# A hand-made order for the head of a linear-attention and SwiGLU kernel, with six zero matmuls fewer

## The chip, the cores and the metric

The kernel runs on one core of one Trainium2 chip. The metric is the device time of one execution in microseconds (us). The times before are 200.81, 200.97 and 201.14, median 200.97.

A core has five engines, each with its own queue that it works through in order: TensorE (PE, matrix products into PSUM), VectorE (DVE), ScalarE (ACT), GpSimd (POOL) and SyncE (SP, which here only issues transfers). [...]

## The reference

A recurrence with a decaying state per head (B = 4 batches, H = 8 heads, S = 768 steps, D = 48), then an RMS norm and a gated feed-forward layer (384 to 1536 to 384).

```python
for t in range(S):
    cur = np.einsum('bhd,bhe->bhde', u[None] * kt, vt)
    y[:, :, t] = np.einsum('bhd,bhde->bhe', rt, state + cur)
    state = wt[:, :, :, None] * state + np.einsum('bhd,bhe->bhde', kt, vt)
...
xn = x / rms * rms_g
g = xn @ w_gate
silu = g * (1.0 / (1.0 + np.exp(-g)))
val = xn @ w_val
return (silu * val @ w_out).astype(np.float32)
```

## The kernel before

The 768 steps are cut into six superblocks of 128 steps. A superblock n has four batches j, and its recurrence is computed as masked matrix products. The feed-forward part works on a whole superblock, 4 x 128 = 512 rows at a time, in twelve chunks f of 128 hidden units.

Every step is a small function `fn(n, j)`, and the text constant `ORDER` names all 1086 of them as `fn.n.j`. At its end the kernel runs through that list and calls them, so that this one list sets the order on every engine:

```python
    for step in ORDER.split():
        fn, n, j = step.split(".")
        fns[fn](int(n), int(j))
```

The same list decides the PSUM banks. Three rings, `a` and `b` of two banks and `q` of four, are handed out by `psum`, which takes the bank whose last use lies furthest back in `ORDER`.

The steps for one batch of a superblock, with the engine and the line that the profile shows:

- `load_r`, `load_k`, `load_v` (L248) and `load_w` (L261): transfers, issued on SP.
- `ln` (ACT), `cs_mm` (PE, L402 to L409), `exp_r` and `exp_k` (ACT): the cumulated decay. In superblock 0 the exponentials stay in PSUM; in superblock 1 they are written to SBUF as `er` and `ek`.
- `r_mul` (L455) and `k_mul` (L461), DVE: r and k times the decay, into `rk`. `w_tot` (L446), DVE.
- `rk_pe` (PE, L484) and `rk_tr` (ACT, L493): the transpose of `rk`, and its copy into `rkT`.
- `q_mm` (PE, L502 and L504): the score products; `q_mask_e` (L509) and `q_mask_o` (L517), DVE: their masks, into `qts`.
- `bonus_mul` (POOL, L467 and L468, two products of about 1.0 us), `bonus_sum` (DVE, L472), `bonus_v` (POOL, L477): the u term, into `ydiag`.
- `x_pe` (PE, L557) puts `ydiag` into the output bank; `y_mm` (PE, L552) adds the score products.
- `x_sq` (L570), `x_rstd`, `xn_mul` (L585), ACT: the norm. `xn_pe` (PE, L596) and `xn_out` (DVE, L607): the transpose of the normed rows into `xnt`.
- `cast_v` (ACT, L379), `st_mm` (PE, L530), `st_new` (DVE, L537): the state for the next superblock.

When `xn_out` of all four batches is done, the feed-forward part can start: `gate_mm` and `val_mm` (PE, L626, three matmuls each), `silu` (ACT), `h_mul` (DVE, L658), and later `o_mm` (PE, L672). `load_gv.g.h` (L351) and `load_wo` (L357) bring the weights in; they are issued on POOL, whose queue they share with the products above. `gate_mm.0.0` needs `load_gv.0.0`; chunks 4 to 11 need `load_gv.1.0` and `load_gv.1.1`.

`warm` (L374) is a matmul of zeros whose result nobody reads. There are 13 at the start (L285), outside the list, and 36 in the list, all in superblock 0's part. The step's first number counts them and has no other meaning.

The head, in this text, is the stretch up to the first `gate_mm` and `val_mm` of superblock 0, about the first 36 us. In it the list mixes steps of superblock 0 with the first ones of superblock 1.

Of the kernel before, what the change touches and what calls it, by code (L numbers as in the profile page):

```python
# [25 lines left out]
load_w.0.1 load_r.0.1 load_w.0.0 warm.21.0 warm.31.0 load_k.0.1 load_k.0.0 load_w.0.2 load_k.0.2 ln.0.1 load_r.0.0  # L26
load_w.0.3 ln.0.0 load_r.0.2 warm.22.0 load_v.0.0 load_v.0.1 warm.4.0 load_r.0.3 load_k.0.3 load_v.0.3 cs_mm.0.1
warm.9.0 exp_k.0.1 load_v.0.2 cs_mm.0.0 load_r.1.0 load_k.1.3 load_k.1.0 load_r.1.1 exp_r.0.1 ln.0.2 k_mul.0.1
load_k.1.1 load_r.1.3 warm.29.0 warm.13.0 r_mul.0.1 load_r.1.2 load_k.1.2 exp_r.0.0 w_tot.0.1 load_v.1.0 load_v.1.1
load_v.1.3 rk_pe.0.1 r_mul.0.0 load_v.1.2 warm.5.0 exp_k.0.0 bonus_mul.0.1 bonus_mul.0.0 warm.12.0 k_mul.0.0 w_tot.0.0  # L30
# [15 lines left out]
val_mm.0.1 h_mul.0.3 silu.0.9 gate_mm.0.6 q_mm.1.0 bonus_sum.1.3 silu.0.6 gate_mm.0.7 q_copy_o.1.1 q_copy_o.1.0
q_mask_o.1.0 q_mask_o.1.1 gate_mm.0.5 rk_pe.1.3 bonus_v.1.0 h_mul.0.1 silu.0.7 val_mm.0.7 load_r.2.2 q_mask_e.1.0
load_wo.0.0 val_mm.0.6 q_mask_e.1.1 rk_tr.1.3 r_mul.1.2 gate_mm.0.11 k_mul.1.2 h_mul.0.7 cast_v.1.0 y_mm.1.0
load_wo.1.0 silu.0.5 cast_v.1.1 bonus_v.1.1 val_mm.0.9 rk_pe.1.2 h_mul.0.6 st_mm.1.0 st_mm.1.1 silu.0.11 val_mm.0.5
x_add.1.0 x_sq.1.0 h_mul.0.9 cast_v.1.2 val_mm.0.4 gate_mm.0.4 gate_mm.0.8 rk_tr.1.2 silu.0.4 st_new.1.0 st_new.1.1  # L50
q_mm.1.2 bonus_mul.1.2 load_wo.2.0 cast_v.1.3 q_copy_o.1.2 h_mul.0.5 silu.0.8 gate_mm.0.10 q_mask_o.1.2 h_mul.0.4
q_mask_e.1.3 val_mm.0.8 y_mm.1.1 st_mm.1.2 bonus_sum.1.2 q_copy_o.1.3 silu.0.10 bonus_v.1.3 st_mm.1.3 val_mm.0.11
q_mask_o.1.3 q_mask_e.1.2 h_mul.0.8 x_add.1.1 load_k.2.1 x_rstd.1.0 ln.2.0 x_sq.1.1 y_mm.1.3 h_mul.0.11 val_mm.0.10
bonus_v.1.2 x_add.1.3 y_mm.1.2 h_mul.0.10 x_rstd.1.1 x_add.1.2 xn_mul.1.0 x_sq.1.3 cs_mm.2.0 st_new.1.3 o_mm.0.0
x_rstd.1.3 ln.2.1 x_sq.1.2 load_v.2.1 xn_pe.1.0 cs_mm.2.1 ln.2.2 xn_mul.1.1 x_rstd.1.2 cs_add.2.0 xn_out.1.0 o_out.0.0
st_new.1.2 xn_mul.1.2 o_mm.0.2 cs_add.2.1 xn_pe.1.1 exp_r.2.0 r_mul.2.0 bonus_mul.2.0 exp_r.2.1 xn_pe.1.2 load_v.2.0
o_mm.0.1 w_tot.2.0 xn_out.1.2 cs_mm.2.2 exp_k.2.0 ln.2.3 xn_mul.1.3 w_tot.2.1 r_mul.2.1 load_k.2.2 load_k.2.3 exp_k.2.1
cs_mm.2.3 xn_out.1.1 xn_pe.1.3 cs_add.2.2 cs_add.2.3 k_mul.2.0 exp_r.2.2 o_mm.0.3 xn_out.1.3 k_mul.2.1 exp_r.2.3
cast_v.2.1 r_mul.2.2 bonus_mul.2.1 w_tot.2.2 o_out.0.2 exp_k.2.3 gate_mm.1.7 out_dma.0.0 val_mm.1.7 st_mm.2.1 rk_tr.2.0
exp_k.2.2 r_mul.2.3 w_tot.2.3 gate_mm.1.1 val_mm.1.1 k_mul.2.3 st_new.2.1 load_v.2.2 rk_tr.2.1 silu.1.7 gate_mm.1.5  # L60
k_mul.2.2 h_mul.1.7 silu.1.1 load_v.2.3 gate_mm.1.6 silu.1.5 val_mm.1.5 silu.1.6 h_mul.1.1 o_out.0.3 load_r.3.0
bonus_sum.2.1 load_w.3.1 bonus_mul.2.2 gate_mm.1.3 val_mm.1.6 o_out.0.1 gate_mm.1.0 h_mul.1.5 val_mm.1.0 bonus_sum.2.0
q_mm.2.0 silu.1.0 h_mul.1.6 cast_v.2.0 cast_v.2.2 val_mm.1.3 q_copy_o.2.0 q_mask_e.2.0 st_mm.2.0 q_copy_o.2.1 rk_tr.2.3
bonus_v.2.1 q_mask_o.2.0 h_mul.1.0 silu.1.3 st_new.2.0 q_mask_e.2.1 h_mul.1.3 gate_mm.1.2 st_mm.2.2 q_mask_o.2.1
silu.1.2 val_mm.1.2 y_mm.2.0 load_w.3.0 gate_mm.1.4 y_mm.2.1 gate_mm.1.10 bonus_v.2.0 rk_tr.2.2 h_mul.1.2 val_mm.1.4
silu.1.4 x_add.2.0 silu.1.10 x_add.2.1 st_new.2.2 gate_mm.1.9 gate_mm.1.8 val_mm.1.9 q_mm.2.2 h_mul.1.4 x_sq.2.1
x_sq.2.0 bonus_mul.2.3 load_r.3.1 silu.1.9 out_dma.0.3 gate_mm.1.11 cast_v.2.3 x_rstd.2.0 val_mm.1.11 x_rstd.2.1
load_k.3.0 bonus_sum.2.2 h_mul.1.9 q_mask_e.2.3 load_k.3.1 silu.1.8 load_v.3.0 q_copy_o.2.2 q_copy_o.2.3 q_mask_o.2.2
silu.1.11 ln.3.0 q_mask_e.2.2 load_w.3.3 q_mask_o.2.3 bonus_v.2.2 h_mul.1.11 load_w.3.2 ln.3.1 bonus_sum.2.3 st_mm.2.3
val_mm.1.10 y_mm.2.3 y_mm.2.2 val_mm.1.8 xn_mul.2.0 bonus_v.2.3 out_dma.0.2 h_mul.1.10 out_dma.0.1 load_r.3.3 cs_mm.3.0  # L70
x_add.2.2 h_mul.1.8 cs_add.3.0 o_mm.1.1 cs_mm.3.1 x_add.2.3 load_r.3.2 x_sq.2.2 load_v.3.2 load_k.3.2 st_new.2.3 ln.3.3
exp_r.3.0 x_sq.2.3 ln.3.2 x_rstd.2.2 w_tot.3.0 exp_k.3.0 xn_mul.2.2 xn_pe.2.0 xn_mul.2.1 cs_add.3.1 x_rstd.2.3 o_mm.1.0
xn_out.2.0 exp_r.3.1 exp_k.3.1 r_mul.3.0 o_out.1.0 k_mul.3.0 xn_pe.2.2 cs_mm.3.3 cs_add.3.3 k_mul.3.1 bonus_mul.3.1
w_tot.3.1 xn_mul.2.3 o_mm.1.3 rk_tr.3.0 xn_pe.2.1 xn_out.2.2 r_mul.3.1 bonus_mul.3.0 exp_r.3.3 o_out.1.1 out_dma.1.0
r_mul.3.3 cs_mm.3.2 cs_add.3.2 xn_pe.2.3 exp_k.3.2 rk_tr.3.1 w_tot.3.3 k_mul.3.2 exp_r.3.2 load_w.5.2 xn_out.2.3
xn_out.2.1 exp_k.3.3 r_mul.3.2 bonus_sum.3.1 load_k.4.2 o_out.1.3 o_mm.1.2 gate_mm.2.5 w_tot.3.2 val_mm.2.1
bonus_sum.3.0 o_out.1.2 bonus_v.3.0 cast_v.3.0 val_mm.2.0 cast_v.3.2 bonus_mul.3.2 out_dma.1.3 silu.2.5 gate_mm.2.0
q_mm.3.0 q_mask_e.3.0 load_k.3.3 silu.2.0 h_mul.2.0 load_v.3.1 gate_mm.2.1 silu.2.1 gate_mm.2.11 val_mm.2.5 h_mul.2.1
q_mask_e.3.1 silu.2.11 cast_v.3.1 rk_tr.3.2 st_mm.3.2 gate_mm.2.2 q_copy_o.3.0 k_mul.3.3 load_w.4.0 silu.2.2
q_copy_o.3.1 h_mul.2.5 st_new.3.2 q_mask_o.3.0 val_mm.2.2 gate_mm.2.3 gate_mm.2.4 st_mm.3.0 h_mul.2.2 silu.2.4  # L80
# [644 lines left out]
```

## Time and profile before

| what | value |
|---|---|
| median of three runs | 200.97 us |
| the profiled execution's own time | 201.61 us |
| its span, first to last instruction | 199.9 us |
| PE busy | 192.6 us, 96% of the span |
| DVE busy | 151.6 us, 76% |
| ACT busy | 136.9 us, 69% |
| POOL busy | 125.5 us, 63% |
| mean granted TensorE clock | 0.999 |

The shares are means over a head, a long steady part and a tail. The steady part is filled by PE; the head is not, and there the engines take turns at being waited for. How the stretches of the head look, in us of work per stretch:

| stretch, us | PE | DVE | ACT | POOL |
|---|---|---|---|---|
| 16.9 to 20.0 (3.1) | 2.00 | 1.57 | 2.45 | 2.01 |
| 22.5 to 25.0 (2.5) | 2.50 | 2.50 | 2.44 | 1.59 |
| 25.0 to 27.5 (2.5) | 2.50 | 1.88 | 1.70 | 2.40 |
| 27.5 to 30.0 (2.5) | 2.39 | 2.50 | 2.47 | 2.42 |
| 30.0 to 36.0 (6.0) | 5.60 | 6.00 | 5.11 | 3.54 |

PE's numbers here contain the zero matmuls, so that a full PE is not a PE with work to do. An instruction's duration runs from its start to its end, and instructions that follow each other on one engine overlap by about a tenth of a microsecond; so the distance from one start to the next is the better measure of what an instruction costs its engine.

### The profile page before, as it was taken

The numbers are of one execution on the slowest core, as the hardware profiler recorded it, in microseconds if no ns is written. First come the engines' busy times: TensorE is split into PE (matmuls) and PEld (weight loads), VectorE is DVE, ScalarE is ACT, GpSimd is POOL, SyncE is SP. The second block draws the span as 40 slices with busy tenths as digits, with TensorE's granted clock in tenths as the row PEclk, the third lists the DMA queues.
The fourth block names the chain that finished last, engine by engine and source line by source line (L and its number), as shares of the span: only waits on it lengthen the run. The fifth ranks groups of instructions, "written<-read, shape, count | busy, mean of one in ns | idle before, by whom it ended". The sixth has DMA issues, their size and how long they took to land.

```text
span 199.9 us, 4406 instructions
## 1 busy us (share of the span) xinstructions
PE 192.6 (96%) x1577; PEld 113.7 (57%) x1577; DVE 151.6 (76%) x290; ACT 136.9 (69%) x279; POOL 125.5 (63%) x184
## 2 busy tenths in 40 slices
PE   7996999999999999999999999999999999999994
...
PEclk9999999999999999999999999999999999999999
...
GB/s 153 254 228 161 196 215 209 201 180 187 191 173 237 209 164 210 241 156 249 218 152 210 233 211 180 196 188 108 115 147 229 40 25 59 0 157 43 0 59 100
DMA packets 121566, 32.41 MB, mean 162 GB/s; under 512 B 116420, under 2 KB 120392, under 8 KB 121544
## 3 DMA queue, kind: packets, MB, share of 16 engines
...
q0 software_dynamic: 2032, 3.54, 9.9%
...
## 4 chain that ended last, share of the span: by engine, by line
PE 77%; SPq 6%; DMA 6%; DVE 5%; POOL 3%; issue 1%; ACT 0%; DVEq 0%
PE ps_av L626 10%; PE ps_bu L626 10%; PE ps_bv L626 10%; PE ps_au L626 10%; PE ps_qz L672 6%; PE ps_qu L672 6%; PE ps_qv L672 5%; PE ps_qx L672 5%; SPq L248 4%; DMA wo_sb<-in_moe_w_out_dram 4%; DMA kt<-in_k_dram 2%; SPq L261 2%; DVE rk L461 2%; POOL qts L520 1%; PE ps_bv L557 1%
## 5 line engine op out<-in xcount | busy, mean ns | idle before, releaser
L672 PEld LDWEIGHTS <-ht 128*128 128x128 bf16 x300 | 28.3, 98 | 17.3 <-issue 0.7
L235 ACT ACTIVATE sg<-ps_av 128x512 bf16<-128x512 f32 x37 | 22.2, 599 | 21.1 <-PE ps_av L626 18.5
L626 PEld LDWEIGHTS <-wg_sb 128*128 128x128 bf16 x216 | 23.0, 114 | 18.8 <-DVE wcol L451 0.2
L626 PEld LDWEIGHTS <-wv_sb 128*128 128x128 bf16 x216 | 22.8, 114 | 18.8 <-issue 0.9
L467 POOL TENSOR_TENSOR ruk<-rt,kt 128x384 f32<-128x384 f32 x24 | 24.4, 1016 | 9.9 <-DMA rt<-in_r_dram 5.0
L626 PE MATMUL ps_av<-xnt,wg_sb 128*128 128x512 bf16 x111 | 30.1, 380 | 0.0
L626 PE MATMUL ps_bu<-xnt,wv_sb 128*128 128x512 bf16 x108 | 29.3, 380 | 0.5 <-DVE ht L658 0.5
L658 DVE TENSOR_TENSOR ht<-ps_bu,sg 128x512 bf16<-128x512 f32 x36 | 24.7, 687 | 6.2 <-PE ps_bu L626 4.2
L658 DVE TENSOR_TENSOR ht<-ps_bv,sg 128x512 bf16<-128x512 f32 x36 | 24.7, 685 | 6.1 <-PE ps_bv L626 5.7
L626 PE MATMUL ps_bv<-xnt,wv_sb 128*128 128x512 bf16 x108 | 29.2, 379 | 0.0
L626 PE MATMUL ps_au<-xnt,wg_sb 128*128 128x512 bf16 x105 | 28.5, 380 | 0.0
L235 ACT ACTIVATE sg<-ps_au 128x512 bf16<-128x512 f32 x35 | 20.9, 596 | 9.7 <-PE ps_au L626 8.4
L468 POOL TENSOR_TENSOR ruk<-ruk,u_bc 128x384 f32<-128x384 f32 x24 | 24.2, 1009 | 1.9
L477 POOL TENSOR_TENSOR ydiag<-vt,diag 128x384 f32<-128x384 f32 x24 | 20.1, 842 | 1.1 <-DVE diag L472 1.1
L520 POOL TENSOR_SCALAR_AFFINE_SELECT qts<-qts 128x512 bf16<-128x512 bf16 x20 | 13.1, 663 | 11.9 <-ACT qts L513 11.8
L461 POOL TENSOR_TENSOR rk<-kt,ek 128x384 bf16<-128x384 f32 x16 | 15.9, 1006 | 1.7 <-DMA kt<-in_k_dram 0.9
L235 ACT ACTIVATE lw<-wt 128x384 bf16<-128x384 f32 (+1 forms) x20 | 11.3, 580 | 4.9 <-DMA wt<-in_w_dram 4.9
L233 ACT ACT_TABLE_LOAD x10 | 12.8, 1283 | 1.8 <-PEq L709 1.6
L672 PE MATMUL ps_qz<-wo_sb,ht 128*128 128x384 bf16 (+1 forms) x84 | 13.8, 314 | 0.0
L472 DVE TENSOR_REDUCE diag<-ruk 128x8 f32<-128x384 f32 x24 | 12.9, 542 | 0.7 <-POOL ruk L468 0.7
L672 PE MATMUL ps_qx<-wo_sb,ht 128*128 128x384 bf16 x72 | 12.8, 326 | 0.4 <-DMA wo_sb<-in_moe_w_out_dram 0.4
L672 PE MATMUL ps_qu<-wo_sb,ht 128*128 128x384 bf16 x72 | 12.7, 326 | 0.0
...
## 6 DMA issues: line engine op xcount, KB each, us to landing
...
```

The lines of the kernel that those rows point to most:

```text
L233: nc.scalar.preload_act_table_set(table_name)
L235: return nc.scalar.activation(**kw).ins
L248: dmas["load_" + which, n, j] = nc.sync.dma_start(out=inp[which, n, j], in_=t[j, :, n * L:(n + 1) * L, :].rearrange("h t d -> t h d")).ins
L461: eng.tensor_tensor(out=rk[:, n % 2, j, 1, :, 0:D], in0=inp["k", n, j], in1=bank["cs_k", n, j][:, 0:DM].rearrange("p (h d) -> p h d", h=H) ...
L467: nc.gpsimd.tensor_tensor(out=ruk[n, j], in0=inp["r", n, j], in1=inp["k", n, j], op=ALU.mult)
L468: nc.gpsimd.tensor_tensor(out=ruk[n, j], in0=ruk[n, j], in1=u_bc, op=ALU.mult)
L472: nc.vector.tensor_reduce(out=diag[n, j].rearrange("p h o -> p (h o)"), in_=ruk[n, j], axis=mybir.AxisListType.X, op=ALU.add)
L477: nc.gpsimd.tensor_tensor(out=ydiag[n, j], in0=inp["v", n, j], in1=diag[n, j].to_broadcast([128, H, D]), op=ALU.mult)
L520: nc.gpsimd.affine_select(out=qts[n, j][:, 1], in_=qts[n, j][:, 1], compare_op=ALU.is_gt, fill=0.0, base=0, pattern=[[0, NP], [1, 128]], c ...
L626: nc.tensor.matmul(ps[:, cols], lhsT=units(ws, c, f), rhs=xnt[n][:, c, cols], start=(first and c == 0), stop=(c == KC - 1))
L658: nc.vector.tensor_tensor(out=ht[n][:, f, :], in0=bank.pop(("v", n, f)), in1=bank.pop(("sg", n, f)), op=ALU.mult)
L672: nc.tensor.matmul(ps[:, cols], lhsT=ht[n][:, f, b * L:(b + 1) * L], rhs=wo_sb[:, f, cols], start=(f == 0), stop=(f == FC - 1))
```

## The change

Only the list `ORDER` differs. Its first 79 steps, to `cs_mm.0.3`, are the same but for the numbers of the `warm` steps; the part from there to the first expert matmuls is rewritten; from `val_mm.0.0` on, 883 steps are the same. The list has 1080 steps, 30 of them `warm`. In the rewritten part, steps of superblock 0 stand in front of those of superblock 1 on each engine.

```diff
-load_k.2.0 cs_mm.0.3 exp_r.0.3 exp_k.0.3 r_mul.0.2 bonus_v.0.0 q_mask_o.0.1 w_tot.0.2 q_mm.0.0 warm.26.0 bonus_v.0.1
-cs_mm.1.0 rk_pe.0.2 cast_v.0.1 q_mask_e.0.1 exp_r.1.0 q_mask_e.0.0 warm.7.0 load_r.2.1 warm.27.0 k_mul.0.3 warm.23.0
-exp_k.1.0 warm.8.0 warm.19.0 rk_tr.0.2 cast_v.0.3 x_pe.0.1 cast_v.0.2 r_mul.0.3 w_tot.0.3 bonus_sum.0.2 rk_pe.0.3
-q_mm.0.2 load_r.2.0 q_mask_o.0.2 y_mm.0.1 bonus_mul.0.3 rk_tr.0.3 x_pe.0.0 q_mask_o.0.0 load_gv.0.0 q_mask_e.0.2
-x_sq.0.1 cs_mm.1.1 y_mm.0.0 exp_r.1.1 load_w.2.3 bonus_v.0.2 warm.3.0 warm.20.0 bonus_sum.0.3 x_rstd.0.1 warm.15.0
-x_sq.0.0 load_r.2.3 x_pe.0.2 y_mm.0.2 q_mm.0.3 warm.6.0 warm.14.0 xn_mul.0.1 bonus_v.0.3 warm.17.0 load_gv.0.1
-x_rstd.0.0 r_mul.1.0 x_sq.0.2 warm.2.0 warm.33.0 warm.25.0 k_mul.1.0 xn_mul.0.0 load_gv.1.0 x_pe.0.3 warm.16.0
-q_mask_e.0.3 q_mask_o.0.3 st_mm.0.0 warm.30.0 y_mm.0.3 exp_k.1.1 bonus_mul.1.0 bonus_mul.1.1 xn_pe.0.1 st_mm.0.3
-x_rstd.0.2 st_new.0.0 warm.35.0 r_mul.1.1 warm.11.0 cs_mm.1.3 x_sq.0.3 warm.28.0 xn_pe.0.0 xn_out.0.1 xn_out.0.0
-warm.0.0 st_new.0.3 xn_mul.0.2 x_rstd.0.3 exp_k.1.3 xn_mul.0.3 xn_pe.0.2 cs_mm.1.2 xn_out.0.2 xn_pe.0.3 xn_out.0.3
-st_mm.0.2 rk_pe.1.0 st_mm.0.1 k_mul.1.1 exp_r.1.3 exp_r.1.2 st_new.0.2 exp_k.1.2 rk_tr.1.0 k_mul.1.3 gate_mm.0.0
-val_mm.0.2 st_new.0.1 gate_mm.0.3 rk_pe.1.1 bonus_sum.1.0 silu.0.0 load_gv.1.1 val_mm.0.0 gate_mm.0.2 silu.0.3 silu.0.2
+load_k.2.0 cs_mm.0.3 r_mul.0.2 q_mask_o.0.1 q_mm.0.0 warm.15.0 w_tot.0.2 exp_r.0.3 q_mask_e.0.1 cs_mm.1.0 bonus_v.0.0
+exp_k.0.3 q_mask_e.0.0 cast_v.0.1 rk_pe.0.2 bonus_v.0.1 exp_r.1.0 q_mask_o.0.0 warm.16.0 load_r.2.1 warm.17.0 warm.18.0
+warm.19.0 warm.20.0 warm.21.0 warm.22.0 exp_k.1.0 rk_tr.0.2 k_mul.0.3 bonus_mul.0.3 q_mm.0.2 r_mul.0.3 x_pe.0.1
+cast_v.0.3 w_tot.0.3 bonus_sum.0.2 rk_pe.0.3 y_mm.0.1 x_pe.0.0 y_mm.0.0 q_mask_o.0.2 q_mask_e.0.2 rk_tr.0.3 load_gv.0.0
+load_gv.0.1 cast_v.0.2 load_r.2.0 q_mm.0.3 bonus_sum.0.3 x_sq.0.1 cs_mm.1.1 warm.23.0 q_mask_e.0.3 q_mask_o.0.3
+exp_r.1.1 load_w.2.3 x_rstd.0.1 bonus_v.0.2 x_sq.0.0 bonus_v.0.3 r_mul.1.0 x_pe.0.2 warm.24.0 load_r.2.3 warm.25.0
+warm.26.0 xn_mul.0.1 k_mul.1.0 y_mm.0.2 x_rstd.0.0 load_gv.1.0 x_pe.0.3 x_sq.0.2 y_mm.0.3 bonus_mul.1.0 xn_mul.0.0
+xn_pe.0.1 st_mm.0.0 warm.27.0 xn_out.0.1 st_new.0.0 exp_k.1.1 x_rstd.0.2 xn_pe.0.0 st_mm.0.3 cs_mm.1.3 x_sq.0.3
+xn_out.0.0 st_new.0.3 xn_mul.0.2 warm.28.0 load_gv.1.1 xn_pe.0.2 rk_pe.1.0 warm.29.0 st_mm.0.2 x_rstd.0.3 xn_out.0.2
+bonus_mul.1.1 xn_mul.0.3 st_new.0.2 exp_k.1.3 exp_r.1.3 xn_pe.0.3 cs_mm.1.2 exp_k.1.2 exp_r.1.2 xn_out.0.3 r_mul.1.1
+gate_mm.0.0 gate_mm.0.3 k_mul.1.1 st_mm.0.1 val_mm.0.2 silu.0.0 rk_pe.1.1 k_mul.1.3 rk_tr.1.0 st_new.0.1 bonus_sum.1.0
+val_mm.0.0 gate_mm.0.2 silu.0.3 silu.0.2
```

More of the change, by code (lines that the diff above doesn't have):

```diff
@@ L25 @@
 ORDER = """
[L26 to L30, printed above, removed]
@@ L46 @@
[L46 to L50, printed above, removed]
@@ L51 @@
[L51 to L80, printed above, removed]
@@ L81 @@
-val_mm.2.4 load_v.3.3 y_mm.3.0 gate_mm.2.6 bonus_v.3.1 silu.2.3 st_new.3.0 st_mm.3.1 bonus_mul.3.3 h_mul.2.4 x_add.3.0
-silu.2.6 cast_v.3.3 load_v.4.0 st_new.3.1 bonus_sum.3.2 gate_mm.2.7 val_mm.2.3 x_sq.3.0 gate_mm.2.10 q_mask_o.3.1
-h_mul.2.3 rk_tr.3.3 val_mm.2.6 load_k.4.1 q_mm.3.2 val_mm.2.7 load_w.4.1 h_mul.2.6 silu.2.10 silu.2.7 val_mm.2.10
-q_mask_e.3.3 x_rstd.3.0 load_r.4.1 h_mul.2.7 bonus_v.3.2 gate_mm.2.8 q_copy_o.3.2 q_copy_o.3.3 cast_v.4.0 st_mm.3.3
-gate_mm.2.9 q_mask_o.3.3 bonus_sum.3.3 load_w.4.3 bonus_v.3.3 h_mul.2.10 load_k.5.3 y_mm.3.1 q_mask_e.3.2 val_mm.2.8
@@ L91 @@
-k_mul.4.0 ln.4.2 r_mul.4.1 w_tot.4.0 xn_pe.3.3 xn_out.3.1 cs_mm.4.3 out_dma.1.1 r_mul.4.0 load_r.5.2 cs_mm.4.2
-k_mul.4.1 rk_tr.4.0 bonus_mul.4.3 cast_v.4.1 o_out.2.1 bonus_sum.4.2 bonus_v.4.1 cs_add.4.3 xn_pe.3.2 xn_out.3.3
-exp_r.4.3 rk_tr.4.1 exp_k.4.3 load_w.5.1 o_mm.2.3 cs_add.4.2 xn_out.3.2 val_mm.3.1 r_mul.4.3 exp_r.4.2 load_v.4.2
-w_tot.4.2 bonus_mul.4.0 o_out.2.3 w_tot.4.3 r_mul.4.2 bonus_sum.4.3 exp_k.4.2 o_out.2.2 gate_mm.3.6 st_mm.4.0
-val_mm.3.0 st_new.4.0 k_mul.4.2 gate_mm.3.1 q_mm.4.0 silu.3.6 gate_mm.3.0 silu.3.1 silu.3.0 q_mask_e.4.0 h_mul.3.1
@@ L96 @@
-k_mul.4.3 q_copy_o.4.0 st_mm.4.1 gate_mm.3.4 q_copy_o.4.1 val_mm.3.4 load_r.5.3 bonus_sum.4.0 h_mul.3.0 st_new.4.1
-silu.3.4 q_mask_o.4.0 gate_mm.3.3 val_mm.3.6 y_mm.4.0 bonus_v.4.0 gate_mm.3.8 bonus_mul.5.3 out_dma.2.2 bonus_v.4.2
-h_mul.3.6 silu.3.3 silu.3.8 h_mul.3.4 rk_tr.4.2 q_mask_e.4.1 x_add.4.0 gate_mm.3.2 val_mm.3.8 val_mm.3.3 gate_mm.3.9
-x_sq.4.0 cast_v.4.3 q_mask_o.4.1 h_mul.3.8 silu.3.9 rk_tr.4.3 silu.3.2 bonus_v.4.3 q_mm.4.2 load_r.5.0 val_mm.3.9
-q_copy_o.4.2 gate_mm.3.10 y_mm.4.1 gate_mm.3.7 bonus_sum.5.3 x_rstd.4.0 q_mask_e.4.2 h_mul.3.3 h_mul.3.9 load_k.5.1
@@ new lines @@
+gate_mm.0.9 silu.0.1 bonus_mul.1.3 val_mm.0.1 h_mul.0.3 silu.0.9 gate_mm.0.6 q_mm.1.0 bonus_sum.1.3 silu.0.6
+gate_mm.0.7 q_copy_o.1.1 q_copy_o.1.0 q_mask_o.1.0 q_mask_o.1.1 gate_mm.0.5 rk_pe.1.3 bonus_v.1.0 h_mul.0.1 silu.0.7
+val_mm.0.7 load_r.2.2 q_mask_e.1.0 load_wo.0.0 val_mm.0.6 q_mask_e.1.1 rk_tr.1.3 r_mul.1.2 gate_mm.0.11 k_mul.1.2
+h_mul.0.7 cast_v.1.0 y_mm.1.0 load_wo.1.0 silu.0.5 cast_v.1.1 bonus_v.1.1 val_mm.0.9 rk_pe.1.2 h_mul.0.6 st_mm.1.0
+st_mm.1.1 silu.0.11 val_mm.0.5 x_add.1.0 x_sq.1.0 h_mul.0.9 cast_v.1.2 val_mm.0.4 gate_mm.0.4 gate_mm.0.8 rk_tr.1.2
@@ new lines @@
+silu.0.4 st_new.1.0 st_new.1.1 q_mm.1.2 bonus_mul.1.2 load_wo.2.0 cast_v.1.3 q_copy_o.1.2 h_mul.0.5 silu.0.8
+gate_mm.0.10 q_mask_o.1.2 h_mul.0.4 q_mask_e.1.3 val_mm.0.8 y_mm.1.1 st_mm.1.2 bonus_sum.1.2 q_copy_o.1.3 silu.0.10
+bonus_v.1.3 st_mm.1.3 val_mm.0.11 q_mask_o.1.3 q_mask_e.1.2 h_mul.0.8 x_add.1.1 load_k.2.1 x_rstd.1.0 ln.2.0 x_sq.1.1
+y_mm.1.3 h_mul.0.11 val_mm.0.10 bonus_v.1.2 x_add.1.3 y_mm.1.2 h_mul.0.10 x_rstd.1.1 x_add.1.2 xn_mul.1.0 x_sq.1.3
+cs_mm.2.0 st_new.1.3 o_mm.0.0 x_rstd.1.3 ln.2.1 x_sq.1.2 load_v.2.1 xn_pe.1.0 cs_mm.2.1 ln.2.2 xn_mul.1.1 x_rstd.1.2
@@ new lines @@
+cs_add.2.0 xn_out.1.0 o_out.0.0 st_new.1.2 xn_mul.1.2 o_mm.0.2 cs_add.2.1 xn_pe.1.1 exp_r.2.0 r_mul.2.0 bonus_mul.2.0
+exp_r.2.1 xn_pe.1.2 load_v.2.0 o_mm.0.1 w_tot.2.0 xn_out.1.2 cs_mm.2.2 exp_k.2.0 ln.2.3 xn_mul.1.3 w_tot.2.1 r_mul.2.1
+load_k.2.2 load_k.2.3 exp_k.2.1 cs_mm.2.3 xn_out.1.1 xn_pe.1.3 cs_add.2.2 cs_add.2.3 k_mul.2.0 exp_r.2.2 o_mm.0.3
+xn_out.1.3 k_mul.2.1 exp_r.2.3 cast_v.2.1 r_mul.2.2 bonus_mul.2.1 w_tot.2.2 o_out.0.2 exp_k.2.3 gate_mm.1.7 out_dma.0.0
+val_mm.1.7 st_mm.2.1 rk_tr.2.0 exp_k.2.2 r_mul.2.3 w_tot.2.3 gate_mm.1.1 val_mm.1.1 k_mul.2.3 st_new.2.1 load_v.2.2
@@ new lines @@
+rk_tr.2.1 silu.1.7 gate_mm.1.5 k_mul.2.2 h_mul.1.7 silu.1.1 load_v.2.3 gate_mm.1.6 silu.1.5 val_mm.1.5 silu.1.6
+h_mul.1.1 o_out.0.3 load_r.3.0 bonus_sum.2.1 load_w.3.1 bonus_mul.2.2 gate_mm.1.3 val_mm.1.6 o_out.0.1 gate_mm.1.0
+h_mul.1.5 val_mm.1.0 bonus_sum.2.0 q_mm.2.0 silu.1.0 h_mul.1.6 cast_v.2.0 cast_v.2.2 val_mm.1.3 q_copy_o.2.0
+q_mask_e.2.0 st_mm.2.0 q_copy_o.2.1 rk_tr.2.3 bonus_v.2.1 q_mask_o.2.0 h_mul.1.0 silu.1.3 st_new.2.0 q_mask_e.2.1
+h_mul.1.3 gate_mm.1.2 st_mm.2.2 q_mask_o.2.1 silu.1.2 val_mm.1.2 y_mm.2.0 load_w.3.0 gate_mm.1.4 y_mm.2.1 gate_mm.1.10
@@ new lines @@
+bonus_v.2.0 rk_tr.2.2 h_mul.1.2 val_mm.1.4 silu.1.4 x_add.2.0 silu.1.10 x_add.2.1 st_new.2.2 gate_mm.1.9 gate_mm.1.8
+val_mm.1.9 q_mm.2.2 h_mul.1.4 x_sq.2.1 x_sq.2.0 bonus_mul.2.3 load_r.3.1 silu.1.9 out_dma.0.3 gate_mm.1.11 cast_v.2.3
+x_rstd.2.0 val_mm.1.11 x_rstd.2.1 load_k.3.0 bonus_sum.2.2 h_mul.1.9 q_mask_e.2.3 load_k.3.1 silu.1.8 load_v.3.0
+q_copy_o.2.2 q_copy_o.2.3 q_mask_o.2.2 silu.1.11 ln.3.0 q_mask_e.2.2 load_w.3.3 q_mask_o.2.3 bonus_v.2.2 h_mul.1.11
+load_w.3.2 ln.3.1 bonus_sum.2.3 st_mm.2.3 val_mm.1.10 y_mm.2.3 y_mm.2.2 val_mm.1.8 xn_mul.2.0 bonus_v.2.3 out_dma.0.2
@@ new lines @@
+w_tot.3.3 k_mul.3.2 exp_r.3.2 load_w.5.2 xn_out.2.3 xn_out.2.1 exp_k.3.3 r_mul.3.2 bonus_sum.3.1 load_k.4.2 o_out.1.3
+o_mm.1.2 gate_mm.2.5 w_tot.3.2 val_mm.2.1 bonus_sum.3.0 o_out.1.2 bonus_v.3.0 cast_v.3.0 val_mm.2.0 cast_v.3.2
+bonus_mul.3.2 out_dma.1.3 silu.2.5 gate_mm.2.0 q_mm.3.0 q_mask_e.3.0 load_k.3.3 silu.2.0 h_mul.2.0 load_v.3.1
+gate_mm.2.1 silu.2.1 gate_mm.2.11 val_mm.2.5 h_mul.2.1 q_mask_e.3.1 silu.2.11 cast_v.3.1 rk_tr.3.2 st_mm.3.2
+gate_mm.2.2 q_copy_o.3.0 k_mul.3.3 load_w.4.0 silu.2.2 q_copy_o.3.1 h_mul.2.5 st_new.3.2 q_mask_o.3.0 val_mm.2.2
@@ new lines @@
+gate_mm.2.3 gate_mm.2.4 st_mm.3.0 h_mul.2.2 silu.2.4 val_mm.2.4 load_v.3.3 y_mm.3.0 gate_mm.2.6 bonus_v.3.1 silu.2.3
+st_new.3.0 st_mm.3.1 bonus_mul.3.3 h_mul.2.4 x_add.3.0 silu.2.6 cast_v.3.3 load_v.4.0 st_new.3.1 bonus_sum.3.2
+gate_mm.2.7 val_mm.2.3 x_sq.3.0 gate_mm.2.10 q_mask_o.3.1 h_mul.2.3 rk_tr.3.3 val_mm.2.6 load_k.4.1 q_mm.3.2 val_mm.2.7
+load_w.4.1 h_mul.2.6 silu.2.10 silu.2.7 val_mm.2.10 q_mask_e.3.3 x_rstd.3.0 load_r.4.1 h_mul.2.7 bonus_v.3.2
+gate_mm.2.8 q_copy_o.3.2 q_copy_o.3.3 cast_v.4.0 st_mm.3.3 gate_mm.2.9 q_mask_o.3.3 bonus_sum.3.3 load_w.4.3
```

90 lines of the change are left out of this document (55 added, 35 removed).

## The prediction

> **What bounds the kernel now.** I read the page's slices first, then the chain of waits, then the timeline engine by engine from 13 to 60 us, because everything the change touches runs before 36 us.
>
> The page's busy tenths, 40 slices of 5 us, show that TensorE (PE) is not full in the first slices only. The granted clock (PEclk) is 9 tenths or more in every slice.
>
> ```profile
> span 199.9 us, 4406 instructions
> ...
> PE   7996999999999999999999999999999999999994
> ...
> PEclk9999999999999999999999999999999999999999
> ```
>
> The chain of waits (start, length, what; all in us) shows what sets the head's end. Until 18.6 us it is the SP queue and the arrival of k for superblock 0, batch 3. After that it zigzags through PE, and from 27 to 36 us it is VectorE (DVE) without a break; PE takes over at 36.09.
>
> ```profile
> 13.71 4.91 DMA kt<-in_k_dram
> ...
> 27.31 1.34 DVE rk L455
> 28.65 0.93 DVE xnt L607 x2
> 29.58 0.46 DVE st L537
> ...
> 30.90 1.88 DVE rk L461
> 32.78 0.47 DVE st L537
> 33.25 0.81 DVE rk L461
> ...
> 36.09 0.81 PE ps_bu L626 x3
> ```
>
> The timeline (start, duration, instruction) shows why those DVE products are long. L455 and L461 take 0.55 where one factor lies in PSUM, and here 1.34, 1.88 and 0.88.
>
> ```profile
> 24.55 0.81 POOL L351 DMA_DIRECT2D wv_sb<-in_moe_w_val_dram  x1
> ...
> 27.24 1.00 POOL L468 TENSOR_TENSOR ruk<-ruk,u_bc 128x384 f32<-128x384 f32 x1
> 27.31 1.34 DVE L455 TENSOR_TENSOR rk<-rt,er 128x384 bf16<-128x384 f32 x1
> 28.19 1.31 POOL L467 TENSOR_TENSOR ruk<-rt,kt 128x384 f32<-128x384 f32 x1
> ...
> 32.43 1.20 POOL L468 TENSOR_TENSOR ruk<-ruk,u_bc 128x384 f32<-128x384 f32 x1
> 33.17 0.88 DVE L461 TENSOR_TENSOR rk<-kt,ek 128x384 bf16<-128x384 f32 x1
> ```
>
> For superblock 1 both factors are in SBUF, and such a product ends about 0.55 after the running GpSimd (POOL) product has ended, while the next POOL product stretches (1.31, 1.20 instead of 1.00): the two engines take turns. From 36.09 PE is almost gapless to the end; its only wait up to 55 us is 0.44 at 54.35 for the third part of `wo_sb`.
>
> **The change, part by part.** SP's queue is the same, instruction for instruction. After the first 31 steps of PE, 20 of ScalarE (ACT) and 14 of DVE, and up to the first expert matmuls, the order differs; on POOL two weight loads move forward. PSUM banks of these steps are renamed; after about 36 us all queues are as before.
>
> *Six zero matmuls.* In a row they start 0.16 to 0.22 apart (24.55, 24.72, 24.94, 25.10, 25.32, 25.48): 6 x 0.18 = 1.1 us of PE. None of it counts: PE waits in this stretch (1.10 at 19.41), and what it feeds waits for DVE. Without that cover it would be -1.1.
>
> *Weight loads earlier.* val's first part moves before two `bonus_v`, its second before `bonus_mul.1.1`. The first part of gate is issued at 20.76 and lands 5.9 later, at 26.7; the next was issued at 24.55 and lands 6.3 later (30.9), the third at 25.36 and lands at 35.3, the fourth at 30.52 and lands at 39.9. Each was issued before its predecessor landed, so this queue was never empty: landings stay, cost and gain 0. On POOL the cost is a place in the queue: 0.81 in front of `bonus_v.0.2`.
>
> *The path to the first expert matmul.* `rk_tr.0.3` goes in front of `cast_v.0.2`: `rk_pe.0.3` can start at 19.8 (after the product at 19.18, 0.55), ends at 20.4; copy 1.01, to 21.46 (before: 22.0). `q_mm.0.3` no longer stands behind `y_mm.0.2`: 21.5 instead of 24.22. DVE then runs without its 0.84 pause: `q_mask_o.0.2` 20.20, `q_mask_e.0.2` 20.80, `bonus_sum.0.3` 21.40, masks of batch 3 21.95 and 22.55 (0.60 each), `r_mul.1.0` 23.15. POOL: loads 20.76 and 21.79, `bonus_v.0.2` 22.60 to 23.44 (before 21.79). So `x_pe.0.2` starts at 23.5 instead of 23.28; 0.65 for it and 3 x 0.17 for zero matmuls put `y_mm.0.2` at 24.65, its end at 25.0, and ACT's `x_sq.0.2` at 25.02 (before 24.64). From there ACT is a chain by its own spacings: 0.46 + 0.46 + 0.37 + 0.34 + 0.11 = 1.74 to `x_sq.0.3` (26.76; before 27.24, waiting for PE), then 0.46, 0.46, 0.32, 0.11 to `xn_mul.0.3` at 28.11 (before 28.99, with `exp_k.1.3` ahead, now behind: 0.37). It ends at 28.68. PE has `rk_pe.1.0` (0.45), one zero matmul (0.16) and `st_mm.0.2` (0.2) ahead of `xn_pe.0.3`: 28.9. DVE does `st_new.0.2` (0.47) first, `xn_out.0.3` at 29.54, ready at 30.08; `gate_mm.0.0` starts at 30.2 instead of 31.12. That alone would be -0.9.
>
> *What is late next.* `r_mul.1.1` was moved from 27.31 to behind `xn_out.0.3`, so DVE now has `r_mul.1.1`, `k_mul.1.1`, `k_mul.1.3` in a row from 30.01, while it stands idle from about 25 to 26.2, waiting for `xn_pe.0.1`. Queued behind the three are `st_new.0.1`, two `bonus_sum` and `h_mul.0.0`, which frees the bank that `val_mm.0.3` needs: the wait that ended at 36.09. POOL at that time: `bonus_v.0.3` to 24.8 (0.84, plus 0.44 if `r_mul.1.0`, at 23.15 blocked until 23.44, gets in between), gate load 0.78, `bonus_mul.1.0` 2.04, val load 0.82, `bonus_mul.1.1` from 28.35 to 30.4, then `bonus_mul.1.3`. Taking turns as the rows above do: `r_mul.1.1` waits to 30.4 and ends at 30.9; POOL to 31.85; `k_mul.1.1` to 32.35; POOL to 33.3; `k_mul.1.3` to 33.8, against 34.05 before: **-0.25**. Without the 0.44 POOL is that much earlier and the same sum ends at 33.4: **-0.65**. PE reaches `rk_pe.1.1` at 30.2 + 0.65 + 0.65 + 0.2 + 0.65 = 32.35, so it does not stand there. After `k_mul.1.3` the DVE row is unchanged, 1.31 to `h_mul.0.0`. I take **-0.4**, nearer the first end, since 23.15 against 23.44 is a narrow margin.
>
> [...]
>
> *Downstream.* From 36.1 to 39 PE is full, at 40.61 POOL waits for ACT, which waits for `q_mm.1.0`: all of it shifts. The loads of `wo_sb` are issued that much earlier; around 40 to 42 us the DMA share is 0.77 against 1.05 to 1.1 before it, so there is room for them. If there is none, PE's wait at 54.35 grows by what PE gained, and nothing is left: bounds 0 and -0.4; I take -0.4, since the chain there is an issue time plus 7.23.
>
> **Sum.** Span 199.9 - 0.4 = 199.5. The profiled run took 201.61, 1.71 more than its span, so 201.2 in its terms; the median of the runs shown is 200.97, so **200.6 us**.
>
> **Rivals.**
> 1. *DVE gets past POOL.* If one of the three products meets an idle POOL, its stall (up to 0.9) goes too, until PE is the bound: 30.2 plus six expert matmuls, `st_mm` and the transposes (6 x 0.65 + 0.2 + 0.45) puts `val_mm.0.3` at 34.8 to 35.1, so -0.7 to -1.3: 199.9 to 200.2. For it: POOL has only one `bonus_mul` left at 30.4. Against it: that one lies exactly over the three products.
> 2. *POOL comes late.* If `bonus_mul.1.1` starts at 29.2 or later instead of 28.35 (k or r of superblock 1 landing late, since before it was used at 28.19 with landings about 5.5 after issues at 20.45 and 21.49; or load issues longer than 0.81), four POOL products lie over three DVE ones: each waits a whole 1.0. 30.0 + 3 x (1.0 + 0.5) = 34.5 against 34.05, and `rk_pe.1.1` holds PE too: +0.5, so 201.5. Against it: the data queues keep their order.
> 3. *Hidden at `wo_sb`*: 201.0, as above.
> 4. *The clock falls.* The rows show full clock even from 16.9 to 20.0, where PE was busy 2.00 of 3.10 us; the longest new hole is 0.8 (22.7 to 23.5). In the first 5 us, zero matmuls at a lower rate start 0.32 apart, later 0.16, so one slow stretch of 3 us in the head costs up to 1.5 more: 202.5. [...]
>
> **How the numbers follow.** A measurement of this kernel can tell about 0.2% (0.4 us) from no change. Forecast 40%, rival 1 33%, rival 2 17%, rival 3 7%, clock 3%. Faster by more than 0.2% (under 200.57): all of rival 1 and about a fifth of the forecast's, 0.41. Slower (over 201.37): rivals 2 and 4 and a little of the rest, whose later 160 us may fall differently, 0.22. Within: 0.37. The range 199.9 to 201.5 takes in rivals 1 to 3 and both ends of the DVE sum; the forecast's own is 200.3 to 200.9.
>
> **What would show it.** Right: `gate_mm.0.0` near 30.2, the three DVE products each lengthened between 30 and 34, `val_mm.0.3` near 35.7, and PE shifted by the same amount at 60 us. Wrong: a product of 0.55 among the three (rival 1); `bonus_mul.1.1` after 29.2 or PE waiting at `rk_pe.1.1` (rival 2); a longer wait at the first `o_mm` (rival 3); zero matmuls 0.32 apart after 10 us (rival 4).

## The result, and the profile after

The changed kernel took 207.39 us (median of six runs: 203.03, 203.72, 207.31, 207.48, 207.50, 207.97); the kernel before took 201.3 in the same session. Four of the six, the profiled one among them, ran with TensorE's granted clock at 0.983 to 0.992, the two shortest with the full clock; the ratio of the comparison, 1.0104 with a 95% interval of 1.0061 to 1.0146, rests on those two alone. The forecast was 200.6, faster; the kernel became slower, by about 2 us in those two, which have no trace, and by about 6 us in the others.

The profiled execution took 207.48 us. Its page shows where to look: the seventh to ninth of its 40 slices (5.1 us each, from 31 us on). PE's row falls to 3 and 5 tenths in the seventh and eighth, its clock to 5 and 8 in the eighth and ninth.

```profile
span 205.8 us, 4375 instructions
...
PE   7998983599999999999999999999999999999994
...
PEclk9999999589999999999999999999999999999999
```

PE's timeline (start, duration, instruction, and in brackets the idle time before it and what ended it) shows both. `gate_mm.0.0` comes at 30.16, where it was forecast (30.2). Then PE stands for 5.59 us in the middle of `rk_pe.1.1` (L483; every line is one lower than before): its first four matmuls need r of superblock 1, batch 1, the other four k. Behind the hole three expert products (gate or val, three matmuls each) take 1.49 and stand 1.28 apart instead of 0.81 and 0.65.

```profile
30.16 0.81 PE L625 MATMUL ps_au<-xnt,wg_sb 128*128 128x512 bf16 x2 [0.31 <-DVE xnt L606]
...
32.27 0.39 PE L483 MATMUL ps_qv<-ident,rk 128*128 128x128 bf16 x4
38.25 0.61 PE L483 MATMUL ps_qv<-ident,rk 128*128 128x128 bf16 x4 [5.59 <-DVE rk L460]
38.65 1.49 PE L625 MATMUL ps_bu<-xnt,wv_sb 128*128 128x512 bf16 x3
39.93 1.49 PE L625 MATMUL ps_au<-xnt,wg_sb 128*128 128x512 bf16 x3
41.21 1.49 PE L625 MATMUL ps_av<-xnt,wg_sb 128*128 128x512 bf16 x3
42.49 0.90 PE L625 MATMUL ps_bu<-xnt,wv_sb 128*128 128x512 bf16 x3
```

The second `ps_bu` there is `val_mm.0.3`, at 42.49 against 36.09 before: +6.4, of which +5.9 are left in the span (205.8 against 199.9). The chain of waits names what the hole waits for. It is one transfer: k of superblock 1, batch 1 (`load_k.1.1`), issued at 21.22 and landed 16.32 us later.

```profile
20.43 0.74 SPq L247
...
21.22 16.32 DMA kt<-in_k_dram
...
37.63 0.57 DVE rk L460
...
38.25 0.61 PE ps_qv L483 x4
38.86 1.28 PE ps_bu L625 x3
```

Before, it was issued at 21.49 and landed 6.3 later, at 27.8; GpSimd used it at 28.19 without a wait. The last number of these lines is the time from issue to landing, before and after:

```profile
kt<-in_k_dram SPq DMA_DIRECT2D x1, 192.0 KB, 6.3
```

```profile
kt<-in_k_dram SPq DMA_DIRECT2D x1, 192.0 KB, 16.3
```

The bytes by queue show why. q0 carries the weights that POOL issues (3.54 MB in all on the page, three times 384 x 1536 numbers of 2 bytes), q1 the loads of SP. The columns are packets, MB and the time that the packets took, as a share of 16 engines. First 26 to 28 us before, then the same two microseconds after, then 30 to 36 us after:

```profile
q1 hardware_dynamic: 1891, 0.36, 88.3%
q0 software_dynamic: 117, 0.11, 41.3%
```

```profile
q0 software_dynamic: 321, 0.32, 95.1%
q1 hardware_dynamic: 317, 0.06, 26.4%
```

```profile
q0 software_dynamic: 550, 1.09, 96.0%
q1 hardware_dynamic: 549, 0.10, 15.9%
```

In these two stretches of the changed kernel, with data on both queues, they got about the same number of packets: 321 and 317, 550 and 549. (Of the windows of 2 us from 24 to 36 us after, only 28 to 30 does not fit, with 200 of weights to 295.) But a packet of r, k or v has 192 bytes (0.36 MB / 1891; 48 numbers of 4), and a packet of weights has 1 KB (first parts: 0.32 MB / 321) or 2 KB (second parts: 1.09 / 550). So SP's loads got 0.06 MB in 2 us, a sixth of what they got before. Before, weights were issued at 20.76, 24.55, 25.36 and 30.52; the first was through by 26.7, the data of the next had hardly begun (0.01 MB from 26 to 27 us), and in that pause SP's loads had the engines nearly to themselves (0.25 MB in the same microsecond). After, they are issued at 20.32, 21.32, 23.69 and 26.75, and the pause is gone.

### The profile page after: what moved, and what is told of

It reads as the page before. It is cut to its first block, busy times and chain, and to the rows that moved or that the text cites. A ratio compares the mean times of both kernels' runs of the same rounds, so it can differ in the third digit from the quotient of the medians.

```text
span 205.8 us, 4375 instructions
## 1 busy us (share of the span) xinstructions
PE 192.9 (94%) x1551; PEld 113.5 (55%) x1571; DVE 151.1 (73%) x290; ACT 137.0 (67%) x279; POOL 125.3 (61%) x184
## 3 DMA queue, kind: packets, MB, share of 16 engines
q0 software_dynamic: 2032, 3.54, 9.4%
## 4 chain that ended last, share of the span: by engine, by line
PE 79%; SPq 9%; DMA 8%; issue 1%; DVE 0%; ACT 0%; DVEq 0%
PE ps_bu L625 12%; PE ps_av L625 12%; PE ps_au L625 11%; PE ps_bv L625 11%; DMA kt<-in_k_dram 8%; SPq L247 8%; PE ps_qz L671 6%; PE ps_qx L671 6%; PE ps_qu L671 6%; PE ps_qv L671 5%; SPq L260 2%; PE ps_qx L501 1%; PE ps_av L416 1%; PE ps_au L416 1%; PE ps_qz L551 1%
```

## The experiments

The edits are shown as the order of GpSimd's steps (once TensorE's, once a piece of code), one step per line; all other queues keep their order. A time in brackets is the range of the runs, a ratio is to the kernel before, with its 95% interval. The kernel before stood at 201.04 beside the kernels with both loads back, with only the loads moved, with six zero matmuls fewer and with the hole filled; at 201.81 beside those with one load back and with all weights later; at 200.91 beside the three with gate's loads moved, and at 200.88 beside the last.

**The new order with val's two loads at their old places.**

```diff
 load_gv.0.0
-load_gv.0.1
 bonus_v.0.2
 bonus_v.0.3
+load_gv.0.1
 load_gv.1.0
 bonus_mul.1.0
-load_gv.1.1
 bonus_mul.1.1
+load_gv.1.1
```

> The changed kernel with val's two weight loads at their old places in POOL's queue (0.1 behind bonus_v.0.3, 1.1 behind bonus_mul.1.1); the rest of the new order and the 30 zero matmuls stay. Theory A (the weight loads, issued without a pause, starve the loads of k and r of superblock 1, whose late k.1.1 holds DVE and PE from 32.6 to 38 us): k.1.1 lands before 28.5 us again, no wait of DVE for it, clock 1.00 throughout, gate_mm.0.0 still near 30.2, median 200.0 to 201.2. Theory B (six zero matmuls fewer let the clock fall): still 203 or more, with a clock under 1.00 between 30 and 42 us. Theory C (the new order of the products on DVE and POOL is itself the loss): 202 to 203.5 with full clock.

Measured: 201.43 us (200.09 to 203.72, 12 runs), ratio 1.0019 [0.9992, 1.0046]. The loss is gone, so the two moves of loads cause it and the rest of the rewritten list does not, though the median is a little above the 200.0 to 201.2 that were expected. The profiled execution (200.79, span 199.1) comes close to the forecast of the head:

```profile
30.60 3.08 DVE L460 TENSOR_TENSOR rk<-kt,ek 128x384 bf16<-128x384 f32 x2
...
35.72 0.81 PE L625 MATMUL ps_bu<-xnt,wv_sb 128*128 128x512 bf16 x3 [0.58 <-DVE ht L657]
```

`k_mul.1.1` and `k_mul.1.3` take 3.08 together, in turns with POOL, and `val_mm.0.3` starts at 35.72 (forecast 35.7, before 36.09). k.1.1 lands 6.4 after its issue, at 28.0, and POOL waits 0.50 for it: there is little room, and a k.1.1 that lands later in some runs would account for the four above 202; they have no trace, so this is not shown.

**The kernel before with only those two loads moved.** The reverse of the last edit, on the old list.

> The kernel before with only the two weight loads moved as in the change (0.1 directly behind 0.0, 1.1 in front of bonus_mul.1.1). Theory A: k.1.1 or r.1.3 lands 5 to 10 us later than before, DVE waits for it from about 31 to 36 us, 202.5 to 208. Theories B and C: 200.6 to 201.6, no wait for k.1.1.

Measured: 203.79 us (203.47 to 207.81), ratio 1.013 [1.0101, 1.0158]. With the old order of all computing steps and all zero matmuls, the two loads alone cost 2.6 us by the ratio. The timeline of an execution at full clock (203.91) shows the same wait, for a k.1.1 issued at 21.19, so the wait costs time without any fall of the clock:

```profile
35.05 0.56 DVE L461 TENSOR_TENSOR rk<-kt,ek 128x384 bf16<-128x384 f32 x1 [4.24 <-DMA kt<-in_k_dram]
```

**One load back at a time.** First only val's first part back behind `bonus_v.0.3`, then only its second part back behind `bonus_mul.1.1`.

> The changed kernel with val's first weight load alone back behind bonus_v.0.3; its second stays in front of bonus_mul.1.1. Theory A1 (it is the first load, issued directly behind gate's, that closes the pause in the weights' traffic at 26 to 28 us in which k.1.1 and r.1.3 came through): k.1.1 lands before 29 us, 200.1 to 201.8, like e1. Theory A2 (the second load does it): still 203 or more, k.1.1 after 33 us.

> The changed kernel with val's second weight load alone back behind bonus_mul.1.1; its first stays directly behind gate's. Theory A1: still 202.5 to 207.5, k.1.1 after 31 us (it waits until gate's second load has passed, since POOL then stands at bonus_mul.1.1, in front of val's second). Theory A2: 200.1 to 201.8.

Measured: 204.26 us (204.07 to 205.13), ratio 1.0137 [1.01, 1.0173], with k.1.1 landing at 32.8; and 205.62 (204.79 to 205.82), ratio 1.0188 [1.0151, 1.0224], with k.1.1 at 34.9. Neither suffices: each load alone fills enough of the pause. Both theories, that one of the two loads is the culprit, fell.

**Six zero matmuls fewer, nothing else**, on the kernel before (`warm.6`, `14`, `17`, `2`, `33`, `25` left out).

> The kernel before without the six zero matmuls that stand in a row between q_mm.0.3 and x_pe.0.3 (six fewer, as in the change, nothing moved). Theory A: 200.5 to 201.4, clock 1.00 in the head. Theory B: 202 or more with a lower clock. Theory C: as A.

Measured: 201.01 us (200.04 to 202.32, 10 runs), ratio 0.9994 [0.9967, 1.002]: nothing, as forecast, and the clock stayed at 1.0. But in the profiled execution `val_mm.0.3` started at 34.50, 1.6 us before its old time, and the span shrank by 0.3 only. PE's windows at 54 to 60 us (us, busy time, clock, DMA share, GB/s) show where that went, here and then in the kernel before:

```profile
54.00:60.00 6.00, 4.51 (x40) 1.00 0.79 153
```

```profile
54.00:60.00 6.00, 5.65 (x48) 1.00 0.80 156
```

In that window DVE waits 2.02 us, until 57.83, for a transfer of r of superblock 2; PE waits in turn for the `w_tot` that DVE does right behind it. In this execution the head's gain runs into the next late transfer.

**The hole filled.** The changed kernel with 34 zero matmuls in front of `rk_pe.1.1`, so that TensorE does not stand still.

```diff
+warm.30.0
...
+warm.63.0
 rk_pe.1.1
```

> The changed kernel with 34 zero matmuls in front of rk_pe.1.1, about 5.5 us of PE work put into the hole where PE waits for k.1.1. Theory A: k.1.1 still lands near 37.5 us and DVE still waits, but the clock stays at 1.00, so all runs come out near the lower of the two values that the changed kernel showed, 203 to 204; the distance to 207.4 is then the price of the fallen clock. Theory B: back to 201.5 or less. Theory C: the added 5.5 us are not hidden, 207 to 209 with full clock and no long wait for k.1.1.

Measured: 205.76 us (205.48 to 206.81), ratio 1.0251 [1.0217, 1.0284], clock 1.0. Missed: 203 to 204 was expected. The zero matmuls themselves ran until 38.2, while DVE had k.1.1 at 36.02, 1.6 earlier than in the changed kernel (37.63); so PE came to `rk_pe.1.1` as late as in the hole, and about 1.6 us of that is the filling's own. What it does tell is the clock's share: with the same lateness (38.20 against 38.25) and full clock, `val_mm.0.3` starts at 40.58 instead of 42.49. About 1.9 us of the 6.4 are the clock.

```profile
40.58 0.81 PE L628 MATMUL ps_bu<-xnt,wv_sb 128*128 128x512 bf16 x3
```

**All weights later.** Gate's and val's first parts and gate's second behind `bonus_v.0.3`, val's second behind `bonus_mul.1.1`: first in the new order of the computing steps, then in the old one.

> The changed kernel with the weight loads behind the activations: gate's first, val's first and gate's second in one go behind bonus_v.0.3 (issued from about 23.5 us), val's second behind bonus_mul.1.1. Theory A: k.1.1, r.1.3, r.1.2 and k.1.2 land before the weights' packets begin at about 26 us, nothing waits for k.1.1, the spread of the runs is that of the kernel before, and the median is 199.8 to 200.6. Rival (the weights then come too late): PE waits for gate's or val's first weights at 30.2 to 33 us, or for val's second at 40, and the median is 201 to 202.

> The kernel before, its 36 zero matmuls and its order of compute, with the weight loads placed as in e7. If the new order of compute is worth what the head showed in e1 (val_mm.0.3 at 35.7 instead of 36.1), this comes out 0.3 to 0.8 above e7, at 200.4 to 201.2; if the gain of e7 is all due to the loads, it equals e7 within 0.2.

Measured: 202.81 us (201.49 to 203.41, 12 runs), ratio 1.0041 [1.0013, 1.0068], and 203.16 (202.4 to 205.42, 12 runs), ratio 1.0089 [1.0054, 1.0124]. Missed: 199.8 to 200.6 and 200.4 to 201.2 were expected. k.1.1 is in time in both, and now the weights are late, as the rival said: PE waits 0.75 for val's first part and 0.43 for gate's second in the first kernel. The second one's PE timeline:

```profile
33.53 1.47 PE L626 MATMUL ps_bv<-xnt,wv_sb 128*128 128x512 bf16 x3 [2.03 <-DMA wv_sb<-in_moe_w_val_dram]
```

In the kernels run here the pause was paid from one side or the other: by k.1.1 (DVE's 4.24 with only the loads moved) or by the weights (PE's 0.75 and 2.03). Between the two kernels, equal in their loads, the new computing order is ahead by 0.35 us, though their intervals overlap and the clock fell in four of the second's twelve executions (0.990 to 0.992) and in none of the first's.

**Gate's first load further forward.** The first kernel above, with `load_gv.0.0` in front of `bonus_mul.0.3`.

> The new order with val's two weight loads back at their old places (as in the first of these kernels), and gate's first load (load_gv.0.0) one step further forward, in front of bonus_mul.0.3, where GpSimd waits about 1.9 us for k of batch 3. Theory (weights that are queued take all but a tenth of the bytes from the loads beside them): gate's first is issued near 17.5 instead of 21.4, its data runs from about 20.5 to 23.5, the pause behind it is longer, k.1.1 lands before 27.5 instead of 28.0, and the late runs of the first kernel go: median 200.6 (200.3 to 200.9). Rival (the same bytes lie in front of k.1.1 whatever their place): r.1.0 and k.1.0, issued at 20.6 and 21.6, now land beside the weights, 3 us later, k_mul.1.0 and bonus_mul.1.0 wait for them, k.1.1 lands at 28 or later: 201.4 to 202.5.

Measured: 204.61 us (203.95 to 206.49), ratio 1.0199 [1.0157, 1.0242]. The rival came true, and at a higher price (the clock fell as well, to 0.990 to 0.992 in five of the six): weights now travel beside r.1.1, whose issue alone holds SP for 3.67 us, so that k.1.1 is issued at 23.70 instead of 21.60. Four pieces of the chain of waits:

```profile
19.99 3.67 SPq L247
...
23.70 10.11 DMA kt<-in_k_dram
...
33.95 1.38 POOL ruk L466
...
36.54 7.83 DMA wv_sb<-in_moe_w_val_dram
```

Val's second part, which stands behind POOL's wait for k.1.1, is late next. The earlier issue did not cure this here: the loads that went out beside the weights paid, r.1.1 with 3.67 us of SP's time, k.1.1 with 10.11 to its landing.

**Gate's second load later.** Two kernels ran under labels whose expectations describe other edits (gate's first load still earlier). The expectations stand here as they are on record, and these runs do not test them.

> As the kernel before this one, but gate's first load still earlier, in front of bonus_v.0.0 (near 15.8), so that its data falls into 18 to 20 us, where the queues moved only 0.16 MB in 2 us against 0.40 beside it. Theory: the transfers there are free, x_pe.0.1 does not wait for bonus_v (2 us of room), k.1.1 lands before 27: median 200.4 (200.1 to 200.8). Rival (same bytes, other place): k.0.3, issued at 19.0, lands 1 us or more later, which holds bonus_mul.0.3 and the head's path: 201.4 or more.

> As the kernel with gate's first load in front of bonus_v.0.0, and val's first behind bonus_mul.0.3, where gate's first used to be (about 21.4 instead of 23.9). Theory: both first parts are through by about 27, gate's second starts its data at about 27.5 as before, so that k.1.1 (issued 21.6) gets less of the time between 24 and 26 and lands near 28 again: 200.4 to 201.4, no better than with gate's load alone. Rival (the earlier the weights, the better, since the bytes in front of k.1.1 count only once): 200.2 or less.

What ran under the first label is the first kernel above with one more move; under the second, the same with `load_gv.0.0` also in front of `bonus_mul.0.3`:

```diff
-load_gv.1.0
 bonus_mul.1.0
+load_gv.1.0
 bonus_mul.1.1
 load_gv.1.1
```

Measured: 200.83 us (199.5 to 202.82, 12 runs), ratio 0.9983 [0.9962, 1.0003], and 200.91 (200.14 to 202.28, 12 runs), ratio 1.0017 [0.9991, 1.0043]. The first has the lowest ratio of all, and still is not to be told from the kernel before. Its profile shows a head that gains and a later stage that loses. `k_mul.1.1` and `k_mul.1.3` take 1.82 for both, with a load issue instead of a product on POOL beside the start of the first (29.37 to 30.17); `val_mm.0.3` starts at 34.26, 1.83 us earlier than before, and PE's window at 54 to 60 us and DVE's timeline there show it given back, as in the kernel with six fewer:

```profile
54.00:60.00 6.00, 4.63 (x41) 1.00 0.80 153
```

```profile
57.65 0.55 DVE L454 TENSOR_TENSOR rk<-rt,ps_au 128x384 bf16<-128x384 f32 x1 [1.90 <-DMA rt<-in_r_dram]
```

The same product stood at 57.94 in the kernel before. The transfer is r of superblock 2, batch 0; GpSimd, which waits for it too, starts on it at 57.69 here, 57.87 with six fewer and 57.98 before. But it does not always land so late. In the second of these kernels, where `val_mm.0.3` came at 35.30, and in the one with both loads back (35.72), GpSimd started on it at 56.15 and 56.07, DVE's product stood at 57.04 and 57.02 without a wait, and PE was full from 54 to 60 us. Their smaller gains were not given back there; the second kernel's line:

```profile
57.04 0.55 DVE L454 TENSOR_TENSOR rk<-rt,ps_au 128x384 bf16<-128x384 f32 x1
```

**Fewer bytes in front of that transfer.** The first of those two, with zeros written in place of two of `wo_sb`'s three parts, so that this kernel leaves out eight of the twelve chunks of the feed-forward output (not half, as the expectation has it).

```diff
     def load_wo(g, _):
+        if g > 0:
+            nc.gpsimd.memset(wo_sb[:, g * FG:(g + 1) * FG, :], 0.0)
+            return
```

> The kernel of label e10_gate_earliest as it ran (the new order, val's first load behind bonus_v.0.3, gate's second behind bonus_mul.1.0, val's second behind bonus_mul.1.1), without the second and third load of wo_sb: these two parts are filled with zeros on GpSimd, so that half of the feed-forward output is missing and 0.77 MB less go through the DMA engines between about 43 and 53 us. In that kernel val_mm.0.3 came 1.8 us earlier than before (34.26 against 36.09) and TensorE lost it again at 54 to 60 us (4.63 us busy of 6, before 5.65), waiting for r and w of superblock 2. Theory (these loads share the engines with wo_sb's, so the data and not the order sets the time at 58 us): without the two loads r.2.2 lands before 55 instead of 57.6, TensorE is busy at least 5.7 of 6 at 54 to 60, and the gain of the head stays: 199.2 (198.6 to 199.8). Rival (SP's queue waits for buffers that GpSimd frees, whatever wo_sb does): the bonus_mul of superblock 2 still starts after 57, 200.4 to 201.2.

Measured: 200.57 us (200.16 to 201.86, 12 runs), ratio 0.9997 [0.9974, 1.002]. Half of the theory shows: the loads of r for superblock 2 begin to be issued at 44.26 instead of 49.02, the last two of them at 50.13 instead of 53.63, `bonus_mul.2.0` starts at 56.14 without a wait instead of 57.69 after one of 3.66, and PE is full in the window:

```profile
56.14 1.00 POOL L469 TENSOR_TENSOR ruk<-rt,kt 128x384 f32<-128x384 f32 x1
```

```profile
54.00:60.00 6.00, 6.00 (x48) 1.00 0.86 184
```

The other half does not: 199.2 was expected. In the profiled execution (201.81) the head itself was late, with `val_mm.0.3` at 36.56, so it had no gain to keep; the runs fall into two groups (eight at 200.16 to 200.71, four at 201.58 to 201.86), and only one of them has a trace. The full window is no proof either: POOL came to `bonus_mul.2.0` 2.1 us later than in the kernel compared, which takes 2.1 off the wait, and the two kernels above with a full window have all of `wo_sb`. What is shown is that with fewer bytes of `wo_sb` the loads of r are issued earlier than in any of the five traces named here (47.34 to 49.29), and that SP's loads moved 1.21 MB from 42 to 50 us against 0.63; not that the head's gain is kept.

## Why the prediction was wrong

*The weight loads: the step that failed.* "Each was issued before its predecessor landed, so this queue was never empty: landings stay, cost and gain 0." It is wrong twice. The queue did run dry: in the changed kernel weights' data starts about 2.5 us after the issue begins (20.32, first packets between 22.5 and 23). Before, gate's first part, landed at 26.7, and val's, issued at 24.55 to 25.36, left 26 to 28 us nearly free of weights (0.11 MB against 0.32 after). And the sum looked at the weights' own landings only, not at the loads beside them. The cost of 0 measured +2.6 us in the old order; in the new one about +2 at full clock and about +6 where the clock fell as well. With both loads back nothing is left that the interval tells from no change.

*POOL comes late (rival 2).* The right place, rejected with "the data queues keep their order". SP issued its loads in the same order, k.1.1 even 0.27 earlier (21.22 against 21.49); what changed was the share of its queue (0.06 MB from 26 to 28 us against 0.36). The price was wrong as well: +0.5 was worked out for a k about 1 us late. It was 9 us late. The margin had been misread too: "about 5.5" from issue to landing reads 6.5 and 6.3 in the trace before, so that k.1.1 was there only 0.4 ahead of its use.

*Six zero matmuls: 0.* Right in the number, 201.01 against 201.04 for the six alone, but not for its reason: in the profiled execution without them `val_mm.0.3` came 1.6 us earlier, so DVE did not hide them all, and the time was lost at 58 us.

*The path to the first expert matmul.* Right: 30.16 for 30.2, and 30.37 with the loads back; ACT's chain, which sets it, ran as worked out (`x_sq.0.2` at 24.99 for 25.02, `xn_mul.0.3` at 28.23 for 28.11). One step off this path was wrong: DVE's pause stayed, 0.82 in front of batch 3's masks.

*Taking turns of DVE and POOL.* Near where k.1.1 came in time, with the loads back: 3.08 for the two `k_mul` and 35.72 for 35.7. That it agrees to 0.02 is partly luck, since that kernel has a load issue behind `bonus_mul.1.1`, and `r_mul.1.1`, the first of the three, ran beside it in 0.55. "About 0.55" behind the end of POOL's product reads 0.41 to 0.43 in the rows of before (28.65 against 28.24, 32.78 against 32.35, 34.05 against 33.63); the sum used 0.5. In the changed kernel itself the step never came to be: `r_mul.1.1` took 0.55 beside an idle POOL, and the next product waited 7.16 us for k.

*Downstream: "there is room for them".* Right for a gain as small as the forecast's: with the loads back, the `o_mm` wait for `wo_sb` was gone and PE was full from 54 to 60 us. Wrong for more: where `val_mm.0.3` came at 34.50 and 34.26, further than rival 1's 34.8, r of superblock 2 was late in its place, and rival 1's 199.9 to 200.2 did not come. (That range does not follow from 34.8 to 35.1 against 36.09, either: the difference is -1.0 to -1.3, so 199.7 to 200.0.) The share of 0.77 was read at 40 to 42 us; the loads of `wo_sb` are issued from 42.7 on (loads back).

*The clock (rival 4).* It fell, though not for want of zero matmuls: the kernel with six fewer kept 1.0. It fell because PE stood for 5.59 us waiting for k: with zero matmuls in that hole it stayed at 1.0. The price was about 1.9, where up to 1.5 had been said for a slow stretch of 3 us; that was an estimate from the first 5 us of the kernel before, where zero matmuls start 0.32 apart, at a granted clock of 1.00. The low stretch that the trace shows measures 6.82 us; the last section has it, with the idle time before it.

The changed kernel's loss in its profiled execution is thus: head -0.96 up to `gate_mm.0.0`; the hole 5.59; the clock about 1.9; together 6.5, against 6.4 at `val_mm.0.3` (smaller terms, such as the 0.47 that PE waited there before, are left out).
